# Products of the identity tile on TensorE while the modulation weights are loading

## The chip, the cores and the metric

The kernel runs on one core of one Trainium2 chip. The metric is the device time of one execution in microseconds (us); lower is better. In the profile the engines are PE (TensorE, the matrix engine; PEld are its weight loads), DVE (VectorE), ACT (ScalarE), POOL (GpSimd) and SP, which here only starts transfers.

## What is computed

One block with adaptive layer norm. A vector `c` gives six rows of 512 numbers (shift, scale and gate for each of two halves) through `silu(c) @ w_mod`. The first half is a state-space convolution over 2048 positions, the second a feed-forward layer with a squared ReLU.

```python
mod = (silu(c) @ w_mod)                       # 512 -> 6 x 512: sa, ca, ga, sb, cb, gb
h = layernorm(x) * (1 + ca) + sa              # x: 2048 x 512
K = real(sum_n C * exp(dt * A * l) * dt * B)  # 512 channels x 2048 positions, 128 states
y = irfft(rfft(h padded) * rfft(K padded))[:2048] + h * Dskip
x = x + ga * y
h = layernorm(x) * (1 + cb) + sb
x = x + gb * (square(relu(h @ w1 + b1)) @ w2 + b2)    # 512 -> 1792 -> 512
```

All values are float32. The identity tile that the change multiplies is not part of this; the kernel has it for transposes and for spreading a row over the partitions.

## The kernel before

The kernel has three stages. The **head** (to about 60 us) loads the parameters, makes `dt`, the step phases and the table entries, takes the statistics of the 16 row tiles of x (128 x 512 each), makes three of the modulation rows, and normalizes and re-sorts the row tiles. The **convolution** (to about 300 us) makes the kernel's spectrum from exponentials and sines, the transform of the input, their product, and the way back, in 8 groups of 64 channels. The **feed-forward** part takes the rest.

The lines of the head that the change and the prediction touch:

- L512: four products that spread `dt` over the partitions, TensorE's first work. L515 copies the result (ACT).
- L464: the loads of `w_mod`, 1 MB for each modulation row. L637 (`mod_rows`): the three groups of 16 products with them, for ga, ca and sa. L654 makes `gs4` from the first group, L655 `g4` from the second, L656 `s4` from the third (all DVE); L658 spreads `g4` over the partitions into the bank `kg`; L660 (ACT) and L661 (DVE) make `shift` from `s4`.
- L611 to L616: statistics of a row tile (DVE), and their last step for four tiles at a time (POOL).
- `row_pieces` (L673 to L683), 16 times: L673 (DVE) scales a row tile, L675 (ACT) makes the selecting tile `sel`, L677 and L680 (TensorE, one product and 16 column-tiled ones) write one of the three banks `ps`, and the copy L683 (ACT) empties it.
- `parameters` (L534 to L588), once for each half of the channels: a chain that goes to and fro between POOL (L535 to L542, L573 to L588), ACT (L544 to L546, L553, L554, L560 to L563, L570 to L572) and DVE (L534, L547 to L550, L555 to L567, L578). L558 is its reciprocal.
- L804 (ACT): the exponentials for the tables. `kgen_sin` (L823 to L825) writes sines into the two double banks `tg`; nothing uses these before.
- L717, L727, L857 and L875: the products of the convolution stage, column-tiled (64, 64, 32 and 64 columns of the array). L1050 are 32 x 32 tiles.

The order in which an engine takes its instructions isn't that of the code. `keep_order` (L168) puts the instructions into groups and walks through them with costs of its own (`weight`) and a clock of its own for TensorE; of the ready groups of an engine it takes the one with the longest way to the end, to which `urgent` adds a number. What it decides it fixes by dependencies. So an instruction that is added on one engine can change the order on the others. Its clock of TensorE:

```python
    WINDOW = 3413
    levels, busy = [0.5], {}
    ...
    def level(t):
        while len(levels) <= t // WINDOW:
            share = busy.get(len(levels) - 1, 0) / WINDOW
            levels.append(1.0 if share >= (0.475 if levels[-1] == 1 else 0.89) else 0.5)
        return levels[int(t // WINDOW)]
    ...
        g = first[e] if e == "SP" else max((g for g in ready[e] if at[g] <= now + 30), key=lambda g: to_end[g])
```

`whole` names instructions that form one group, `behind` holds pairs of which the second waits for the first. `bank("tg", 2)` hands out the two double banks in turn.

## Time and profile before

| | |
|---|---|
| median of 2 runs | 630.12 us (629.96 to 630.27) |
| the profiled execution | 628.47 us |
| its span, first to last instruction | 626.7 us |
| its mean granted clock of TensorE | 0.991 |
| PE, PEld busy | 575.5 us (92%), 489.7 us (78%) |
| DVE, ACT, POOL busy | 459.5 us (73%), 410.6 us (66%), 466.1 us (74%) |
| instructions | 21607 |

All times of a view are us from the span's start. A row of the timeline has the start, the length, the engine, line and operation, the tile written and the tiles read, how many instructions it merges, and in brackets the idle time ahead of it with what ended it. A product of float32 operands counts as two matmul records. In the page's line of slices each digit is a fortieth of the span (15.7 us) in tenths; PEclk is the clock that TensorE was granted. A row of the windows has a stretch, its length, and then the busy time of each engine.

### The profile page before, as it was taken

The page shows a single profiled execution, that of the slowest core. Times are in us where ns is not written, and L with a number is a line of the kernel's source. Part 1 is how long each engine was busy: PE and PEld are TensorE (multiplying, and loading weights), DVE is VectorE, ACT ScalarE, POOL GpSimd, SP SyncE. Part 2 cuts the span into 40 slices and gives each one's busy share as a digit, 9 for nine tenths or more (in the row PEclk, how much of TensorE's full clock was granted, in tenths as well). Part 3 has the DMA queues.
Part 4 walks back from the last instruction along what each step waited for, and adds up shares of the span by engine and source line. Part 5 has one row for each costly group of instructions (what it writes and reads, how often), then busy time and mean ns, then how long its engine had stood idle before and what let it go on. Part 6 is the DMA issues. An engine that isn't in the chain of part 4 may idle for free.

```text
span 626.7 us, 21607 instructions
## 1 busy us (share of the span) xinstructions
PE 575.5 (92%) x9390; PEld 489.7 (78%) x9390; DVE 459.5 (73%) x714; ACT 410.6 (66%) x780; POOL 466.1 (74%) x380
## 2 busy tenths in 40 slices
PE   1488999899999999998899799999998999999997
PEld 1355998899999999997767577788876887778885
DVE  6798779889688998757689944458999745456733
ACT  4938999979969877624785656545955655555441
POOL 6589799999998998240597997527999888761361
PEclk9979999999999999999999999999999999999999
DMA  8940104230311136255243332013534343211432
GB/s 317 396 150 4 68 5 99 43 70 11 64 38 38 22 86 155 54 174 152 71 121 85 97 111 78 17 35 100 152 118 157 113 121 108 57 35 33 136 100 84
DMA packets 45838, 60.70 MB, mean 97 GB/s; under 512 B 5168, under 2 KB 26544, under 8 KB 45616
## 3 DMA queue, kind: packets, MB, share of 16 engines
q1 hardware_dynamic: 45312, 59.20, 32.2%
q8 instruction: 73, 1.20, 0.8%
q10 hardware_dynamic: 432, 0.14, 0.1%
q14 instruction: 21, 0.17, 0.1%
HBM read 46.74 MB, written 4.19 MB: 81 GB/s over the span
## 4 chain that ended last, share of the span: by engine, by line
PE 50%; DVE 18%; POOL 12%; ACT 10%; issue 5%; DMA 4%; DVEq 0%; POOLq 0%; SPq 0%
PE ac L1165 8%; PE ps L875 6%; PE ps L717 5%; PE ps L727 5%; PE ps L1165 4%; PE ac L1186 3%; PE ac L1188 3%; PE ac L1187 3%; PE kg L857 3%; DVE r L1312 3%; DVE xy L867 2%; DVE p L1198 2%; DMA xy<-w 2%; DMA xy<-xt 2%; ACT tables L804 2%
## 5 line engine op out<-in xcount | busy, mean ns | idle before, releaser
L1134 POOL TENSOR_TENSOR w2r<-xy,w2r 128x512 fp32r<-128x512 f32 x56 | 81.2, 1450 | 68.4 <-ACT w2r L1133 68.4
L727 PE MATMUL ps<-xy,t_sb 128*64 128x64 f32 x2048 | 67.4, 223 | 0.6 <-issue 0.5
L727 PEld LDWEIGHTS ps<-xy,t_sb 128*64 128x64 f32 x2048 | 63.6, 138 | 3.4 <-issue 0.8
L875 PE MATMUL ps<-e_sb,xy 128*64 128x128 f32 (+2 forms) x1152 | 64.1, 266 | 2.2 <-ACT xy L719 1.7
L875 PEld LDWEIGHTS ps<-e_sb,xy 128*64 128x64 f32 x1152 | 58.8, 139 | 4.4 <-ACT xy L719 2.1
L1133 ACT CAST w2r<-xy 128x512 fp32r<-128x512 f32 x56 | 34.7, 620 | 24.3 <-DMA xy<-w 10.8
L719 ACT COPY xy<-ps 128x512 f32<-128x512 f32 x64 | 36.9, 589 | 14.8 <-PE ps L717 14.7
L1157 POOL TENSOR_TENSOR k1t<-xy,k1t 128x1024 fp32r<-128x1024 f32 x14 | 33.8, 2413 | 16.3 <-ACT k1t L1155 16.3
L1186 PE MATMUL ac<-w2r,r 128*128 128x512 f32 x112 | 43.8, 391 | 0.3 <-ACT big L1061 0.3
L1187 PE MATMUL ac<-w2r,r 128*128 128x512 f32 x112 | 43.6, 390 | 0.0
L1188 PE MATMUL ac<-w2r,r 128*128 128x512 f32 x112 | 43.6, 390 | 0.0
L837 POOL TENSOR_TENSOR rtl<-tables 128x1024 f32<-128x1024 f32 x22 | 43.4, 1972 | 0.2
L1165 PE MATMUL ac<-tt,k1t 128*128 128x512 f32 x168 | 42.0, 394 | 0.6
L867 DVE TENSOR_TENSOR xy<-ps,xy 128x512 f32<-128x512 f32 x64 | 39.3, 681 | 1.6 <-PE ps L727 1.1
L1165 PEld LDWEIGHTS ac<-tt,k1t 128*128 128x128 f32 x168 | 31.1, 188 | 9.2 <-DVE xy L1285 3.0
L813 POOL TENSOR_TENSOR rtl<-lo,big 128x1024 int32<-128x1024 int32 x16 | 34.3, 2145 | 3.3 <-ACT tg L825 2.6
L813 POOL TENSOR_TENSOR llph<-lo,big 128x1024 int32<-128x1024 int32 x16 | 34.5, 2158 | 1.4 <-ACT tg L825 1.4
L1187 PE MATMUL ps<-w2r,r 128*128 128x512 f32 x84 | 33.1, 395 | 1.9 <-POOL w2r L1134 1.8
L717 PE MATMUL ps<-d_sb,ksb 128*64 128x128 f32 x512 | 34.0, 274 | 0.6 <-DVE xy L867 0.5
L881 DVE COPY big<-ps 128x256 f32<-128x256 f32 (+1 forms) x66 | 24.0, 408 | 13.7 <-PE ps L875 13.6
L1186 PE MATMUL ps<-w2r,r 128*128 128x512 f32 x84 | 33.6, 400 | 0.0
L717 PE MATMUL ps<-d_sb,big 128*64 128x128 f32 x512 | 32.0, 274 | 1.1 <-ACT big L683 0.7
(276 smaller groups left out, 1684.8 us busy)
## 6 DMA issues: line engine op xcount, KB each, us to landing
xy<-w SPq DMA_DIRECT2D x91, 256.0 KB, 2.8
xy<-xt SPq DMA_DIRECT2D x32, 256.0 KB, 4.4
xy<-xy SPq DMA_DIRECT2D x32, 256.0 KB, 3.4
xy<-w_mod SPq DMA_DIRECT2D x6, 1024.0 KB, 8.5
out_dram<-p SPq DMA_DIRECT2D x16, 256.0 KB, 2.1
t_sb<-c_t SPq DMA_DIRECT2D x1, 2048.0 KB, 10.9
i2c<-c_i SPq DMA_DIRECT2D x4, 512.0 KB, 4.6
big<-prm SPq DMA_DIRECT2D x2, 768.0 KB, 5.8
```

The lines of the kernel that those rows point to most:

```text
L717: nc.tensor.matmul(ps[64 * r : 64 * r + 64, 128 * i : 128 * i + 128], src[:, i], d1_sb[:, r], start=True, stop=True)
L719: copy(dst[:, o // 4], ps.rearrange("p (t m) -> p m t", t=4))
L727: nc.tensor.matmul(ps[64 * r : 64 * r + 64, 64 * i : 64 * i + 64].rearrange("p (h q t) -> p q h t", h=2, t=2), t2_sb[:, 8 * g + i, r], src ...
L813: nc.gpsimd.tensor_tensor(ph.rearrange("p d r (a b) -> p (d r) a b", a=4), bc(low_phase[:, us].rearrange("p d r b -> p (d r) b"), 2, 4), b ...
L837: nc.gpsimd.tensor_mul(am[:, 0, :, 32:96].rearrange("p d (v x) -> p d v x", v=2), bc(et[:, 256 + 8 * d0 : 384 + 8 * d0].rearrange("p (y a) ...
L867: nc.vector.tensor_mul(product_piece(y, g), ps, piece(x, g))
L875: nc.tensor.matmul(ps[64 * m : 64 * m + 64], pairs(y)[:, g, i // 2, 64 * m : 64 * m + 64, i % 2], e1_sb[:, h].rearrange("p (r j) -> p r j" ...
L1134: nc.gpsimd.tensor_sub(to[:, 1], wst, to[:, 0].bitcast(F32))
L1165: nc.tensor.matmul(ps[:, cols], x, y, start=(i == 0 and not onto), stop=(i == 5), skip_group_check=onto)
L1186: pe.append(nc.tensor.matmul(banks[m], r2l[:, ms], hi_, start=(f == 0), stop=False))
L1187: pe.append(nc.tensor.matmul(banks[m], r2h[:, ms], lo_, start=False, stop=False))
L1188: pe.append(nc.tensor.matmul(banks[m], r2h[:, ms], hi_, start=False, stop=(f == NF - 1)))
```

## The change

Right behind L512, 54 products are issued in five forms: weights are a block of the identity tile, the moving operand is 64 columns of it, and the results go to the four banks of `tg`, which nobody reads. `warm(rows, cols, n)` goes n times over the array in tiles of `rows` x `cols`: 12 products of 64 x 128, 12 of 64 x 64, 6 of 128 x 128, 12 of 32 x 128 and 12 of 128 x 64. They wait for the last product of L512, each form is one group, and `urgent` ranks them behind everything else that is ready on TensorE.

```diff
     make_identity(nc, ident)
+
+    whole, in_turn, urgent, behind = {}, set(), {}, []
+    for _ in range(2):
+        bank("tg", 2)
+    banks = [t[:, 512 * i : 512 * i + 512] for t in rings["tg"][0] for i in range(2)]
+
...
     for i in range(4):
-        nc.tensor.matmul(
+        dtm = nc.tensor.matmul(
             dtp[:, 128 * i : 128 * i + 128], dtc[:, i : i + 1].to_broadcast([P, P]), ident, start=True, stop=True)
+
+    def warm(rows, cols, n):
+        for i in range(n):
+            for r in range(0, 128, rows):
+                for c in range(0, 128, cols):
+                    m = nc.tensor.matmul(
+                        banks[r // rows][c : c + cols, 64 * (i % 8) : 64 * (i % 8) + 64], ident[r : r + rows, c : c + cols],
+                        ident[r : r + rows, 0:64], start=True, stop=True).ins
+                    whole[m.name] = f"warm {rows} {cols}"
+                    behind.append((dtm.ins, m))
+                    urgent[m.name] = -1000000
+
+    for rows_, cols_, n in ((64, 128, 6), (64, 64, 3), (128, 128, 6), (32, 128, 3), (128, 64, 6)):
+        warm(rows_, cols_, n)
...
-    urgent, behind, paced = {}, [], []
+    paced = []
...
-    whole, in_turn = {}, set()
```

On TensorE they stand between L512 and the first L637, and the order of the rest of the head is the same there. On the other engines the order changes in places. The lines of the changed kernel are higher by 6 (L491 to L512) and by 20 (L515 to L1034), so L535 is L555 there.

DVE around the reciprocal, before. `gs` and `g` are the scaled modulation rows, `big` holds the parameters:

```order
L547 SCALAR_TENSOR_TENSOR big_86<-big_86 128x4x64
L555 SCALAR_TENSOR_TENSOR big_86<-big_86 128x4x64
L558 RECIPROCAL big_86<-big_86 128x4x64
L654 TENSOR_SCALAR gs_361<-ps_161 128x128
L548 SCALAR_TENSOR_TENSOR big_86<-big_86 128x4x64
L556 TENSOR_TENSOR big_86<-big_86 128x4x64
L655 SCALAR_TENSOR_TENSOR g_362<-ps_162,gs_361 128x128
L557 TENSOR_TENSOR big_86<-big_86 128x4x64
L559 TENSOR_TENSOR big_86<-big_86 128x4x64
```

The same place of DVE in the changed kernel:

```order
L567 SCALAR_TENSOR_TENSOR big_86<-big_86 128x4x64
L575 SCALAR_TENSOR_TENSOR big_86<-big_86 128x4x64
L674 TENSOR_SCALAR gs_417<-ps_163 128x128
L578 RECIPROCAL big_86<-big_86 128x4x64
L568 SCALAR_TENSOR_TENSOR big_86<-big_86 128x4x64
L576 TENSOR_TENSOR big_86<-big_86 128x4x64
L577 TENSOR_TENSOR big_86<-big_86 128x4x64
L675 SCALAR_TENSOR_TENSOR g_418<-ps_164,gs_417 128x128
L579 TENSOR_TENSOR big_86<-big_86 128x4x64
```

The read of the first modulation row has moved ahead of the reciprocal, and that of the second behind L577 (L557 before).

A little later on DVE, before, from the statistics of the ninth row tile (`xy_96`) on; `s` is `s4`:

```order
L611 BN_STATS st_75<-xy_96 128x6
L611 BN_STATS st_76<-xy_96 128x6
L612 BN_AGGR mv_74<-st_75 128x2
L612 BN_AGGR mv_74<-st_76 128x2
L611 BN_STATS st_77<-xy_96 128x6
L612 BN_AGGR mv_74<-st_77 128x2
L611 BN_STATS st_78<-xy_96 128x6
L612 BN_AGGR mv_74<-st_78 128x2
L656 TENSOR_TENSOR s_363<-ps_160,gs_361 128x128
```

And in the changed kernel:

```order
L631 BN_STATS st_75<-xy_96 128x6
L632 BN_AGGR mv_74<-st_75 128x2
L631 BN_STATS st_76<-xy_96 128x6
L632 BN_AGGR mv_74<-st_76 128x2
L693 SCALAR_TENSOR_TENSOR xy_94<-xy_94,mv_74,kg_421 128x512
L631 BN_STATS st_77<-xy_96 128x6
L631 BN_STATS st_78<-xy_96 128x6
L676 TENSOR_TENSOR s_419<-ps_162,gs_417 128x128
```

The scaling of the first row tile (L693, before L673) now stands here, ahead of `s4`; before, it came some 20 rows later, with the second and the third.

POOL behind the first product of the second half's parameters (L521), before; `mv` are the statistics:

```order
L521 TENSOR_TENSOR big_86<-big_86 128x4x64
L581 TENSOR_TENSOR big_86<-big_86 128x4x64
L577 TENSOR_TENSOR big_86<-big_86 128x4x64
L573 TENSOR_TENSOR big_86<-big_86 128x4x64
L574 TENSOR_TENSOR big_86<-big_86 128x4x64
L575 TENSOR_TENSOR big_86<-big_86 128x4x64
L615 TENSOR_SCALAR mv_74<-mv_74 128x4
L577 TENSOR_TENSOR big_86<-big_86 128x4x128 x3
L616 TENSOR_TENSOR mv_74<-mv_74,small 128x4
L535 TENSOR_TENSOR big_86<-big_86 128x4x64
L536 TENSOR_TENSOR big_86<-big_86 128x4x64
```

And in the changed kernel:

```order
L541 TENSOR_TENSOR big_86<-big_86 128x4x64
L555 TENSOR_TENSOR big_86<-big_86 128x4x64
L601 TENSOR_TENSOR big_86<-big_86 128x4x64
L597 TENSOR_TENSOR big_86<-big_86 128x4x64
L593 TENSOR_TENSOR big_86<-big_86 128x4x64
L594 TENSOR_TENSOR big_86<-big_86 128x4x64
L595 TENSOR_TENSOR big_86<-big_86 128x4x64
L635 TENSOR_SCALAR mv_74<-mv_74 128x4
L597 TENSOR_TENSOR big_86<-big_86 128x4x128 x3
L636 TENSOR_TENSOR mv_74<-mv_74,small 128x4
L556 TENSOR_TENSOR big_86<-big_86 128x4x64
```

L535 of before (now L555) has moved from behind the statistics to the second place, ahead of L581 (now L601).

In the convolution stage groups of TensorE change places with their neighbours (L857 with L717, L727 and L875), and rows of DVE, ACT and POOL with them; in the feed-forward stage TensorE's order is the same.

## The prediction

> **What bounds the kernel now.** I read the page first, for the shares of the engines and the slices, then the chain that ended last over the first 60 us, then TensorE alone over the same stretch.

> ```profile
> span 626.7 us, 21607 instructions
> PE 575.5 (92%) x9390; PEld 489.7 (78%) x9390; DVE 459.5 (73%) x714; ACT 410.6 (66%) x780; POOL 466.1 (74%) x380
> PE   1488999899999999998899799999998999999997
> PEclk9979999999999999999999999999999999999999
> ```

> TensorE is busy for 575.5 of 626.7 us, and only the first three or so slices (15.7 us each) are thin. From 60 us on it is the engine that everything waits for:

> ```profile
> 120.00:130.00 10.00, 10.00 (x332) 9.47 (x330) 9.87 (x18) 6.42 (x11) 10.00 (x8) 1.00 0.23 47
> 150.00:160.00 10.00, 10.00 (x310) 9.72 (x299) 9.69 (x15) 9.94 (x27) 9.61 (x11) 1.00 0.36 76
> ```

> Here the first busy number is PE (10.00 of 10.00 us), the last POOL. So a change in the first 50 us is worth what it moves the start of that dense stretch, and no more. What sets that start is in the chain (start, us, what):

> ```profile
> 8.00 0.59 ACT big L515
> 18.58 9.03 ACT tables L804 x48
> 32.56 0.74 POOL big L581
> 41.94 0.72 POOL big L535
> 46.43 0.74 POOL big L541
> 47.20 0.51 ACT big L544
> 49.12 0.48 ACT big L683
> 49.65 0.50 PE ps L677
> ```

> From 8 us to 49 us no product of TensorE is on the chain. ACT's exponentials, then POOL without a gap from 32.56, then ACT's phase steps hold back the copy L683, which frees the bank of the ninth row piece (L677 with L680). TensorE in the same stretch, with the idle time ahead of each row:

> ```profile
> 5.91 2.05 PE L512 MATMUL ps<-ident,dtc 128*128 128x128 f32 x8 [5.91 <-DVE dtc L509]
> 14.71 1.93 PE L637 MATMUL ps<-xy,srep 128*32 128x128 f32 x32 [6.75 <-DMA xy<-w_mod]
> 17.39 1.94 PE L637 MATMUL ps<-xy,srep 128*32 128x128 f32 x32 [0.74 <-DMA xy<-w_mod]
> 24.20 1.62 PE L637 MATMUL ps<-xy,srep 128*32 128x128 f32 x32
> 30.32 0.80 PE L677 MATMUL ps<-shift,pick 128*128 128x512 f32 x1 [4.50 <-DVE shift L661]
> 34.39 1.94 PE L680 MATMUL ps<-xy,big 128*32 128x128 f32 x32 [3.26 <-DVE xy L673]
> 45.11 1.08 PE L680 MATMUL ps<-xy,big 128*32 128x128 f32 x32
> 46.55 1.08 PE L680 MATMUL ps<-xy,big 128*32 128x128 f32 x32
> 49.65 0.50 PE L677 MATMUL ps<-shift,pick 128*128 128x512 f32 x1 [2.02 <-ACT big L683]
> ```

> The hole that the change fills is the 6.75 us ahead of 14.71. The same group L680 takes 1.94 us early and 1.08 us later: half clock and full clock, with a row piece every 1.44 us then (46.55 - 45.11). The windows give the switches (PE busy, granted clock, DMA share, GB/s):

> ```profile
> 28.50:29.00 0.50, 0.00 (x0) 0.78 0.85 360
> 39.00:39.50 0.50, 0.50 (x9) 0.98 1.06 393
> ```

> The clock falls at about 28.8, that is 3.0 us after TensorE stopped (24.20 + 1.62 = 25.8), and rises at about 39.0, 4.6 us after work resumed at 34.39. The 2.02 us hole at 47.6 did not drop it.

> **The added products.** 54 of them, two records each by the profile's count (L512: four products, x8), 108 records. Their price is not in this trace; from rows of other forms: L512 gives 0.256 us a record for a full tile and 128 columns at half clock; L637's 1.94/32 = 0.061 is a quarter of that, so four column tiles run side by side. With 64 columns instead of 128 a full tile costs between 0.128 (in proportion) and 0.256. The cheapest end, with row tiles side by side as well: 12 x 0.128 + 24 x 0.064 + 24 x 0.032 + 24 x 0.064 + 24 x 0.032 = 6.1 us at half clock. The dearest, 0.256 and no two row tiles at once: 12 x 0.256 + 24 x (0.256 + 0.128 + 0.256 + 0.128) = 21.5 us. The nearest rows are these, both 64 columns or several row tiles:

> ```profile
> 283.82 1.90 PE L1050 MATMUL ac<-big,i2c 32*32 32x128 f32 x128
> 71.38 1.10 PE L727 MATMUL ps<-xy,t_sb 128*64 128x64 f32 x32
> ```

> L727 costs 0.034 a record at full clock, so 64 columns go in proportion; L1050 costs 0.015, half of L680's 0.034 with four column tiles, so row tiles overlap too. I take 7 us. [...]

> They start at 5.91 + 2.05 = 7.96. With the 4.6 us of the one rise shown, the clock is up at about 10.5; by then 2.5 of the 7 us are done, and the other 4.5 shrink by 1.08/1.94 to 2.5: the end is at 13.0, ahead of w_mod's 14.71, and at 15.0 if the clock does not rise. Cost on the path: nothing; cover: the w_mod load.

> What a raised clock brings there: L637's first two groups shrink from 1.94 to 1.08. Nothing waits for them. The first is read by L654 on DVE, the second by L655, and both stood behind other DVE work:

> ```profile
> 18.14 1.75 DVE L558 RECIPROCAL big<-big 128x256 f32<-128x256 f32 x1
> 19.81 0.23 DVE L654 TENSOR_SCALAR gs<-ps 128x128 f32<-128x128 f32 x1
> 21.86 0.28 DVE L655 SCALAR_TENSOR_TENSOR g<-ps,gs 128x128 f32<-128x128 f32 x1
> 29.58 0.42 DVE L564 SCALAR_TENSOR_TENSOR big<-big 128x256 f32<-128x256 f32 x1 [1.35 <-ACT big L561]
> 33.51 2.05 DVE L673 SCALAR_TENSOR_TENSOR xy<-xy,mv,kg 128x512 f32<-128x512 f32 x3
> ```

> The groups ended at 16.64 and 19.33, their readers began at 19.81 and 21.86. So the warming as such I cost at 0. The clock is lost again before it matters: with g at about 22.3 (0.4 later, since L557 now stands ahead of it), L658 and the third L637 end near 26, and L677 waits for ACT until 30.3, a hole over the 3.0 us that dropped it before.

> **The moved instructions** are what is left, since the planner, which now believes in a fast TensorE, has dealt the rows anew. On POOL, L535 (now L555) leaves the gapless stretch and goes ahead of L581 (now L601):

> ```profile
> 28.46 0.72 POOL L521 TENSOR_TENSOR big<-big 128x256 f32<-128x256 f32 x1 [0.35 <-DMA big<-prm]
> 32.56 0.73 POOL L581 TENSOR_TENSOR big<-big 128x256 int32<-128x256 int32 x1 [3.38 <-ACT big L571]
> ```

> POOL stands idle for 3.38 us there with L535's operands on hand (L521, the row before, waited for the same load). That takes 0.72 us out of the chain between 32.56 and 47.20. Against it: on DVE the first row's L673 (now L693) goes ahead of s4 (0.68 us, 2.05/3) into the stretch that had 1.35 us to spare at 29.58, and the shift row (0.34) now stands ahead of L564. The spare time takes the first, the second reaches L567 and so L581 with 0.1 to 0.3 us. Net gain on the chain: 0.72 - 0.2 = **0.5 us**. DVE's swaps of L654 with L558 and of L655 with L557 leave the same instructions ahead of L559, which ACT waits for: nothing.

> The early row starts the row pieces at 31.1 instead of 34.39. Piece 0 ends at 33.1, piece 1 waits for its own row until 34.4 and ends at 36.3, piece 2 (0.80 + 1.94) at 39.1, five more at 1.44 each at 46.3, against 47.63 before. The ninth still waits for the copy behind ACT's phase steps, now at 49.15. So these 1.3 us turn into idle time: a hole of about 2.85 us instead of 2.02.

> **Behind 60 us**, DVE, ACT and POOL rows and some groups of TensorE (L857 against L717 and L875) change places between about 115 and 300 us; nothing is added. TensorE is full there, so only its few holes can change:

> ```profile
> PE ps L875 <- ACT xy L719: 1.7, 1, 1.7
> PE kg L857 <- issue: 0.7, 1, 0.7
> PE ac L1050 <- issue: 1.9, 2, 1.4
> q8 instruction: 73, 1.20, 0.8%
> ```

> The first could close (-1.7), a like one could open (+2). The 108 records are less than one more packet of q8 (9390/73 = 129 records each) and shift where its packets end by some 20 records; the holes put down to issue bound that at -1.4 to +1.4. I take 0 for both and keep -2.2 to +2.2 for the range.

> **Sum** against the profiled execution, 628.47 us (span 626.7 and 1.8 around it): 0 for the products, 0 for the clock, -0.5 for POOL, 0 behind: 628.0. The median before is 630.12, 1.65 above that execution; I carry the difference to it: **629.6**.

> **The rivals.**

> *The clock drops in the longer hole.* TensorE idle for 3.0 us dropped it, 2.02 did not; 2.85 lies near the former. The next pieces would then run as the early ones, 0.80 + 1.94 instead of 0.50 + 1.08, for up to the 4.6 us of the rise shown: a loss of 4.6 x (1 - 1.58/2.74) = 1.9, so 630.12 - 0.5 + 1.9 = 631.5. Against it: one fall is all that the trace shows, and 2.85 is shorter than its 3.0. [...]

> *The products outlast the load and hold DVE: slower.* L654 now stands ahead of the reciprocal, so DVE stops if the first L637 is not done by 18.1. With 1.94 for that group the point is an end of the products after 16.2; the slack of 0.7 us left ahead of L564 moves it to about 16.9, and from there each us is a us on the chain. At the dear end with the clock up at 11: 8.0 + 3 + 18.5 x 0.56 = 21.4, then 1.08: DVE held 4.3, minus slack 0.7 and gain 0.5: +3.1, 633.2; without any rise the products end at 29.5, +12, 642. The rows L727 and L1050 speak against it.

> *The new order opens or closes holes behind 60 us*: 629.6 + 2.2 = 631.8, or 629.6 - 2.2 = 627.4. POOL's share there (9.6 of 10) says that a late POOL row reaches TensorE soon; that TensorE is full says that little is to be had.

> *It doesn't raise the clock*, because tiled products count for too little activity: L637 stays at 1.94 at 14.71, no reader waits, and the time is the same 629.6.

> **Numbers.** 629.6 as summed, with or without the rise: 0.46. Clock drop, 631.5: 0.27. Holes open, 631.8: 0.10; holes close, 627.4: 0.10. Products too long: 0.07. The likeliest case with its issue term spans 628.2 to 631.0; the range takes in the drop and both kinds of holes and a part of the long products: 626.6 to 633.2. Two per cent, 12.6 us, is about what a measurement of this kernel tells from no change; no case but the extreme of the long products comes near it: faster 0.01, same 0.97, slower 0.02.

> **What would show it.** The added products between 8 and 14 us, L637 (now L657) at about 1.1 us; L601 on POOL near 32.7 and L564's row on ACT (before L544) near 46.7; the first L680 (now L700) at about 31; the hole ahead of the ninth piece near 2.8 us, with the clock at 1.00 or 0.50 behind it; the dense stretch of the same length. I am wrong if L658 or the reciprocal waits for TensorE at 18 to 24 us, or if TensorE has new holes between 115 and 300 us.

## The result and the profile after

The changed kernel takes **636.62 us** (636.25 to 636.99, two runs) against 630.12: a ratio of 1.0103, with a 95% interval of 1.0060 to 1.0147. It is slower by 6.5 us (3.8 to 9.3 by the interval), less than the two per cent but outside the predicted range of 626.6 to 633.2. The profiled execution took 636.25 us, its span is 634.5 us against 626.7.

The head of the page, as it was shown of before (span, busy time of the engines, slices of TensorE and its granted clock):

```profile
span 634.5 us, 21828 instructions
PE 590.6 (93%) x9498; PEld 503.2 (79%) x9498; DVE 454.9 (72%) x714; ACT 412.4 (65%) x780; POOL 469.2 (74%) x380
PE   6688998999989998999889899999998999999997
PEclk9778998999999999999899899999999999999999
```

The 108 records are there (9498 - 9390). TensorE is busier by 15 us, of which the products are 9.4. In the slices the first two digits go from 1 and 4 to 6 and 6. In the convolution the 7th goes from 9 to 8 and the 8th from 8 to 9 (95 to 127 us), and the 12th and 16th (174 to 190 and 238 to 254 us) go from 9 to 8. First the head, in TensorE's timeline:

```profile
7.88 9.39 PE L525 MATMUL tg<-ident 64*128 64x64 f32 x108
17.20 3.61 PE L657 MATMUL ps<-xy,srep 128*32 128x128 f32 x64
22.94 1.16 PE L678 MATMUL kg<-g,ident 128*128 128x128 f32 x8 [2.13 <-DVE g L675]
24.03 1.93 PE L657 MATMUL ps<-xy,srep 128*32 128x128 f32 x32
49.90 0.50 PE L697 MATMUL ps<-shift,pick 128*128 128x512 f32 x1 [2.36 <-ACT big L703]
52.06 1.94 PE L700 MATMUL ps<-xy,big 128*32 128x128 f32 x32
```

The products ran without a gap from 7.88 to 17.2 and hold the first two groups with `w_mod` back from 14.7 to 17.20. These two take 3.61 us together: 1.94 is the half-clock price of one, so the clock rose only near the end of the second. The first record of the granted clock in this trace is the rise at 20.65; the views print 1.00 for all the time before it, so up to there the clock is read from the length of the rows. At 24.03 it is lost again, as the 1.93 shows, and a second time behind the hole at 49.90. Now the convolution, in windows of 10 us (the first busy number is PE, the last POOL, then the granted clock):

```profile
150.00:160.00 10.00, 8.64 (x319) 7.98 (x317) 8.99 (x17) 6.86 (x10) 9.61 (x9) 1.00 0.15 31
170.00:180.00 10.00, 8.39 (x236) 7.72 (x224) 8.45 (x14) 9.91 (x16) 8.29 (x7) 1.00 0.01 3
230.00:240.00 10.00, 8.68 (x274) 8.34 (x272) 9.97 (x17) 6.62 (x9) 9.69 (x9) 1.00 0.02 3
250.00:260.00 10.00, 8.54 (x252) 8.02 (x254) 8.38 (x13) 9.07 (x12) 9.09 (x7) 1.00 0.29 94
```

The same windows before, where the first is already shown with 10.00:

```profile
170.00:180.00 10.00, 9.95 (x326) 9.26 (x324) 9.07 (x18) 7.04 (x10) 9.30 (x7) 1.00 0.02 3
230.00:240.00 10.00, 10.00 (x312) 9.58 (x310) 8.92 (x16) 4.76 (x9) 8.17 (x6) 1.00 0.42 88
250.00:260.00 10.00, 10.00 (x336) 9.58 (x334) 9.85 (x18) 6.68 (x11) 4.04 (x3) 1.00 0.10 32
```

TensorE now stands idle for 1.3 to 1.6 us in each of the four windows, at full clock. Its rows with longer idle time between 75 and 260 us say for whom it waits:

```profile
102.32 1.79 PE L877 MATMUL kg<-llph 128*32 128x64 f32 x64 [2.69 <-DVE ksb L959]
151.49 2.08 PE L747 MATMUL ps<-xy,t_sb 128*64 128x64 f32 x64 [0.69 <-DVE big L901]
159.51 1.09 PE L747 MATMUL ps<-xy,t_sb 128*64 128x64 f32 x29 [0.67 <-issue]
180.10 3.02 PE L747 MATMUL ps<-xy,t_sb 128*64 128x64 f32 x96 [1.69 <-ACT xy L739]
239.42 1.97 PE L895 MATMUL ps<-e_sb,xy 128*64 128x128 f32 x32 [1.32 <-DVE xy L887]
252.46 0.42 PE L877 MATMUL kg<-rtl 128*32 128x64 f32 x8 [1.46 <-issue]
```

The longest of them, 2.69 us at 102.32, adds nothing to the lateness: the kernel before had holes of 0.75, 0.52 and 1.67 us between 100 and 112 us, and these are gone. The other five are what is new; before, the longest between 115 and 260 us is one of 0.51.

Matching TensorE's instructions of the two profiles one by one, the changed kernel is 1.7 us late from 60 to 140 us apart from a stretch around 100, 3 to 4.5 between 160 and 220, 7.6 at 250, and 7.8 at the end. So the profile puts 1.7 us in the head and 6 us between 140 and 250 us, in the stage where the change adds nothing.

### The profile page after: what moved, and what is told of

Read it like the earlier page. It is cut to its first block, busy times and chain, and to the rows that moved or that the text cites. A ratio compares the mean times of both kernels' runs of the same rounds, so it can differ in the third digit from the quotient of the medians.

```text
span 634.5 us, 21828 instructions
## 1 busy us (share of the span) xinstructions
PE 590.6 (93%) x9498; PEld 503.2 (79%) x9498; DVE 454.9 (72%) x714; ACT 412.4 (65%) x780; POOL 469.2 (74%) x380
## 4 chain that ended last, share of the span: by engine, by line
PE 45%; DVE 18%; POOL 17%; ACT 8%; issue 6%; DMA 4%; DVEq 0%; SPq 0%; POOLq 0%; ACTq 0%
PE ac L1183 8%; PE ps L747 4%; PE ps L1183 4%; PE ps L737 4%; PE ac L1204 3%; PE ac L1206 3%; PE ac L1205 3%; PE ps L895 3%; DVE r L1330 3%; PE kg L877 2%; ACT tables L824 2%; DVE p L1216 2%; POOL big L1082 2%; POOL rtl L857 2%; PE kg L1183 2%
## 5 line engine op out<-in xcount | busy, mean ns | idle before, releaser
L857 POOL TENSOR_TENSOR rtl<-tables 128x1024 f32<-128x1024 f32 x22 | 43.3, 1970 | 0.2
L1183 PEld LDWEIGHTS ac<-tt,k1t 128*128 128x128 f32 x168 | 31.1, 188 | 9.2 <-DVE xy L1303 3.0
L833 POOL TENSOR_TENSOR llph<-lo,big 128x1024 int32<-128x1024 int32 x16 | 34.5, 2154 | 5.2 <-ACT tg L845 5.2
L833 POOL TENSOR_TENSOR rtl<-lo,big 128x1024 int32<-128x1024 int32 x16 | 34.4, 2148 | 5.3 <-ACT tg L845 4.6
L901 DVE COPY big<-ps 128x256 f32<-128x256 f32 (+1 forms) x66 | 24.3, 409 | 16.6 <-PE ps L895 14.7
L1205 PE MATMUL ps<-w2r,r 128*128 128x512 f32 x84 | 33.1, 395 | 1.8 <-POOL w2r L1152 1.8
```

The source lines that it names most:

```text
L833: nc.gpsimd.tensor_tensor(ph.rearrange("p d r (a b) -> p (d r) a b", a=4), bc(low_phase[:, us].rearrange("p d r b -> p (d r) b"), 2, 4), b ...
L857: nc.gpsimd.tensor_mul(am[:, 0, :, 32:96].rearrange("p d (v x) -> p d v x", v=2), bc(et[:, 256 + 8 * d0 : 384 + 8 * d0].rearrange("p (y a) ...
L1183: nc.tensor.matmul(ps[:, cols], x, y, start=(i == 0 and not onto), stop=(i == 5), skip_group_check=onto)
L1205: pe.append(nc.tensor.matmul(banks[m], r2h[:, ms], lo_, start=False, stop=False))
```

## The experiments

Two theories stood first. **O**: the order that the planner (`keep_order`) dealt anew is what costs. **R**: the 108 additional records shift where TensorE's instruction packets end (the page's queue q8 has 73 packets before and 74 with them), and the stalls for the next packet then fall on worse places. In all runs below the kernel before ran on the same chip; its medians there were 628.9 to 629.9, single runs 626.9 to 635.0.

### Products without the new order, and the new order without the products

All products run, but the planner gives them no time and no records, so every engine has the order of before:

```diff
+    unseen = {g for g, il in enumerate(groups) if whole.get(il[0].name, "").startswith("warm")}
+    for g in unseen:
+        takes[g] = [0, 0]
...
-        if e == "PE":
+        if g in unseen:
+            pass
+        elif e == "PE":
```

> All 108 added records are issued, but the planner gives them no time and no records, so every other instruction stands in the order of before. Theory O (the loss lies in the new order): within 1.5 us of before, since the products end before anything that waits for them. Theory R (the loss lies in the records: they move the ends of the instruction packets, and with them the holes put down to issue): 4 to 6 us slower than before, with issue holes as in the changed kernel.

Measured: 629.29 us, ratio 1.0006 (0.9987 to 1.0024).

The reverse: one product of each form runs, five in all, and the planner counts each for all of its form, so that the order is that of the changed kernel:

```diff
+    stands_for = {}   # group of a product -> how many it stands for
...
-            n, t = sum(map(records, groups[g])), now
+            n, t = stands_for.get(g, 1) * sum(map(records, groups[g])), now
...
-        for i in range(n):
-            for r in range(0, 128, rows):
-                for c in range(0, 128, cols):
+        for i in (n - 1,):
+            for r in (128 - rows,):
+                for c in (128 - cols,):
```

> 5 products (10 records) instead of 54 (108), while the planner counts all 54: the order of the changed kernel, nearly without its products. Theory O: about 6 us slower than before, like the changed kernel. Theory R: within 1.5 us of before.

Measured: 638.38 us, ratio 1.0140 (1.0102 to 1.0177). The products cost nothing measurable, nor does the shift of 108 records; the order costs all of it. R falls.

### Which part of the order

Both run all products, walk the plan twice (without and with the products) and splice the two orders on every engine where the head ends, at the first group that reads `d1_sb`:

```diff
+    plain, shifted = walk(False), walk(True)
...
+        queues[e] = s[:k] + p[k:]      # e3_head; e3_late has p[:k] + s[k:]
```

> All products; the order of the changed kernel in the head (up to the first L717 of TensorE), the order of before from there. If the head's new order costs what its trace shows at 62 us, 1.6 us slower than before; if the head is free and the convolution's order costs, within 1 us of before.

Measured: 629.28 us, ratio 1.0003 (0.9983 to 1.0023).

> All products; the order of before in the head, the order of the changed kernel from the first L717 on. If the convolution's order costs, 4 to 6 us slower than before; if the records' shift costs whatever the order, as much as the run with the products alone.

Measured: 637.09 us, ratio 1.0129 (1.0089 to 1.0168). The new order of the head, with the early first row, POOL's moved L555 and the longer hole, is worth nothing measurable in either sense. The late part costs 8 us.

The late part differs in three stretches, with the same groups in each on every engine, and they were run one by one: `e6_A` (140 to 210 us), `e6_B` (210 to 255 us) and later `e6_C` (270 to 300 us). Some rows of DVE, ACT and POOL between about 70 and 115 us have changed places as well. These were not run alone, but by 115 us `e3_late` is no later than the kernel before.

```diff
+    span = {
+        "PE": [(103, 161)],
+        "DVE": [(219, 308)],
+        "Activation": [(163, 231)],
+        "Pool": [(117, 165)],
+        "SP": [(40, 48)],
+    }
...
+        for a, b in span[e]:
+            queues[e][a:b] = s[a:b]
```

> All 108 products run. The order is that of the kernel before except between 140 and 210 us (one stretch of the convolution, 58 of TensorE's groups, 89 of VectorE's, 68 of ScalarE's), where it is that of the changed kernel. Theory 'sum of places' (the cost of the late order is a sum of a few separate places, each an instruction that stands ahead of one which TensorE needs sooner): this stretch gave +2.4 us of lag in the profile of e3_late (from -1.23 before 140 us to +1.16 at 180 to 200), made of a hole on TensorE of 0.82 at 149.9 and one of 1.69 at 178.5; so +2.4 us over the kernel before, about 631.5 if that is 629.1 here. Rival 'spread' (the late order as a whole is tighter or looser, no single place counts, what is lost in a stretch is waited for later anyway): under +1, or the whole +8.

Measured: 632.20 us, ratio 1.0057 (1.0036 to 1.0077). The ratio makes it +3.6 us on the 629.9 there, the medians +2.3. This rests on its six times (631.03 to 635.11): the profiled execution was the fastest of them, and its lag behind `e1_products_only`, 2.2 at 210 to 240 us, is 0.7 at 250 and gone by 400.

> All 108 products run. The order is that of the kernel before except between 210 and 255 us (the next stretch: 45 of TensorE's groups, 73 of VectorE's, 55 of ScalarE's), where it is that of the changed kernel. Theory 'sum of places': this stretch gave +2.9 us of lag in the profile of e3_late (from 0.42 at 210 to 3.3 at 250), so +2.9 over the kernel before, about 632.0. Rival 'carried over' (the stretch is only slow because it starts late and out of step, after the stretch at 140 us): under +1.

Measured: 634.16 us, ratio 1.0077 (1.0058 to 1.0096), +4.9 us by the ratio and +4.2 by the medians.

> All 108 products run; the order of before except between 260 and 300 us (20 rows of VectorE, 10 of ScalarE, 3 of GpSimd, none of TensorE), where it is that of the changed kernel. If the loss is the sum of the stretches: e3_late +8.1, less e6_A's +3.6 and e6_B's +4.8, leaves -0.3: within 1 of the kernel before; by the lag in e3_late's profile there (3.7 at 270, 4.8 at 300) +1.

Measured: 630.24 us, ratio 0.9999 (0.9968 to 1.0031). Two stretches carry the loss, and the third carries none. By the ratios A and B add up to 8.5 against the +8.1 of `e3_late`, by the medians to 6.5 against 8.2, so they make up all or most of it; the rivals "spread" and "carried over", with under +1 for a stretch, fall. In stretch B the trace shows what goes with it. Before (`e1_products_only`, whose lines are those of before plus 25), TensorE makes a group of kernel rows `kg<-rtl` at 212, and `kg<-llph` at 221:

```profile
211.99 1.12 PE L882 MATMUL kg<-rtl 128*32 128x64 f32 x64
221.24 1.12 PE L882 MATMUL kg<-llph 128*32 128x64 f32 x64
```

In `e6_B` (lines of before plus 46) that first group stands behind five more, and the windows of 5 us have the rest (PE, PEld, DVE, ACT, POOL):

```profile
212.54 3.02 PE L773 MATMUL ps<-xy,t_sb 128*64 128x64 f32 x96 [0.49 <-ACT xy L765]
220.74 1.12 PE L903 MATMUL kg<-rtl 128*32 128x64 f32 x64
223.86 1.12 PE L903 MATMUL kg<-llph 128*32 128x64 f32 x64
236.95 1.97 PE L921 MATMUL ps<-e_sb,xy 128*64 128x128 f32 x32 [1.36 <-DVE xy L913]
...
220.00:225.00 5.00, 4.89 (x178) 4.30 (x176) 1.92 (x6) 2.00 (x3) 3.46 (x3) 1.00 0.78 174
235.00:240.00 5.00, 3.64 (x88) 3.33 (x86) 5.00 (x9) 1.86 (x3) 3.14 (x3) 1.00 0.40 84
```

The kernel rows come 8.7 us later (220.74 against 211.99). DVE and ACT are then busy for 1.92 and 2.00 of 5 us at 220 (4.33 and 4.69 in `e1_products_only`), and at 235 DVE is full (5.00 of 5.00, against 4.46) while TensorE waits for it. The lag of `e6_B` against `e1_products_only` goes from -0.5 at 215 to +3.1 at 250 and stays at about 3.2 to the end. This is what the trace shows beside the loss; that this one group's place is the cause was not tested alone.

### Putting single instructions back

In stretch A the trace of `e3_late` offered two instructions that wait ahead of others: on ScalarE the second copy of `kg`, which waits 2.7 us for TensorE ahead of the burst of exponentials, and on VectorE a sum that waits for POOL ahead of two copies. Both were moved back, one after the other:

```diff
+    act = queues["Activation"]
+    act[175], act[176] = act[176], act[175]                # e7_A_copy and e8_A_copy_sum
+    dve = queues["DVE"]
+    dve[221:224] = [dve[222], dve[223], dve[221]]          # e8_A_copy_sum
```

> As e6_A, with one instruction moved by one place: on ScalarE the second copy ksb<-kg behind the sines, which in the changed order stands ahead of the burst of 24 exponentials and waits there 2.68 us for TensorE's kg, goes behind the burst. Theory 'sum of places': the burst starts at about 154.7 instead of 157.4, the sines behind it and the copies xy<-ps come 2.7 earlier, TensorE's hole of 1.69 at 178.5 goes: 1.7 under e6_A, about +0.7 over the kernel before. Rival 'TensorE's or GpSimd's own order' (it is the kg products put behind the two groups before them, or GpSimd's additions in another order): as e6_A within 0.5.

Measured: 638.97 us, ratio 1.0148 (1.0127 to 1.0168).

> As e7_A_copy, with one more instruction moved by two places: on VectorE the 1024-wide sum llph<-llph,tg, which in the changed order stands ahead of two copies big<-ps and waits there 0.83 us for GpSimd, goes behind them. Theory 'sum of places': TensorE's hole of 0.82 at 149.9 goes as well: 0.8 under e7_A_copy, within 0.5 of the kernel before. Rival: as e7_A_copy.

Measured: 639.08 us, ratio 1.0160 (1.0138 to 1.0183). The theory of separate places fell, and badly: the first move does not give 1.7 us back, it costs about 6 more (6.8 by the medians, 5.7 by the ratios), and the second changes nothing. The rival of the first, no change, fell too. ScalarE's and TensorE's timelines of `e7_A_copy` show what happens (lines of before plus 48):

```profile
160.11 5.84 ACT L852 ACTIVATE tables<-big 128x128 f32<-128x128 f32 x24 [2.35 <-POOL rtl L885]
165.71 0.45 ACT L986 COPY ksb<-kg 128x256 f32<-128x256 f32 x1
...
166.50 1.75 PE L905 MATMUL kg<-llph 128*32 128x64 f32 x64 [2.52 <-DVE ksb L987]
170.53 1.98 PE L765 MATMUL ps<-d_sb,ksb 128*64 128x128 f32 x16 [2.28 <-DVE big L929]
```

The burst (L852) could not have started earlier: it overwrites `tables`, which POOL's L885 reads until 160.07 (158.12 + 1.95), because POOL too has a new order. So the copy's wait was all but free, and behind the burst it keeps `kg` full, TensorE stands for 2.52 and 2.28 us, and after that its rows run at half clock (1.98 for x16, as against 1.04 at full). In the changed order ScalarE's late copy and POOL's late reads belong together. In POOL's rows, before:

```profile
150.54 0.71 POOL L789 TENSOR_TENSOR lo<-lo,big 128x256 int32<-128x256 int32 x1
152.22 1.97 POOL L837 TENSOR_TENSOR rtl<-tables 128x1024 f32<-128x1024 f32 x1
```

and in the changed kernel, with two more sums for `tables` (L809, before L789) and a phase step (L833) ahead of the reads:

```profile
152.22 2.25 POOL L809 TENSOR_TENSOR lo<-lo,big 128x256 int32<-128x256 int32 x3
154.55 2.14 POOL L833 TENSOR_TENSOR rtl<-lo,big 128x1024 int32<-128x1024 int32 x1
157.66 1.96 POOL L857 TENSOR_TENSOR rtl<-tables 128x1024 f32<-128x1024 f32 x1
```

The same read of `tables` ends at 159.62 instead of 154.19: 5.4 us later, and 3.8 with the 1.7 taken off that the kernel is late anyway. The burst of the changed kernel starts at 160.38, 0.8 us behind that end, so without the copy's wait it could have gained no more than this.

### One engine's order put back

With every engine's order known for both kernels, they were mixed engine by engine over the three stretches (`queues[e]` from `shifted` on the engines named, from `plain` on the others).

> All 108 products run. In the stretches at 140 to 255 and 270 to 300 us VectorE, ScalarE and GpSimd keep the changed order, and TensorE alone goes back to the order of before (it differs at about a dozen places, above all four groups of kg<-rtl or kg<-llph that the changed order puts behind one to six other groups). Theory P (TensorE's kg products are late, so the kernel rows and all that is made of them are late): most of the +8 goes, within +2 of the kernel before, about 631. Theory Q (GpSimd does the sums for tables ahead of the phase additions, which holds ScalarE's burst): as e3_late within 1.5, about +6.5 to +8, 637. Theory J (each engine's order only suits the others', so a mix is no better than the whole): as e3_late or slower, 637 or more.

Measured: 649.68 us, ratio 1.0323 (1.0298 to 1.0348).

> As e9_pe_before, but GpSimd alone goes back to the order of before and TensorE, VectorE and ScalarE keep the changed one. P: as e3_late, +6.5 to +8. Q: most of it goes, within +2, about 631. J: as e3_late or slower.

Measured: 647.90 us, ratio 1.0300 (1.0271 to 1.0329).

> As e9_pe_before, and GpSimd too goes back to the order of before: only VectorE and ScalarE keep the changed order. P: as e9_pe_before, within +2. Q: within +2. J: as e3_late or slower. A theory V (VectorE's and ScalarE's own order costs): +6 to +8.

Measured: 657.24 us, ratio 1.0436 (1.0411 to 1.0462).

> All 108 products run, the order of before on every engine but GpSimd, which has the changed order in those stretches (24 rows). P: 0 to +1, about 630. Q: +4 to +8, 634 to 638. J: anything from +2 up.

Measured: 645.76 us, ratio 1.0244 (1.0222 to 1.0266). P, Q and V all fall, and J holds: each of the four mixes is slower than the whole new order, so neither TensorE's nor POOL's part is the loss by itself. VectorE's and ScalarE's parts were run together only. Of the mix with POOL's changed rows alone, TensorE's longest waits:

```profile
160.61 1.15 PE L773 MATMUL ps<-xy,t_sb 128*64 128x64 f32 x32 [3.09 <-DVE xy L913]
185.57 5.50 PE L773 MATMUL ps<-xy,t_sb 128*64 128x64 f32 x128 [4.31 <-ACT xy L765]
239.25 3.68 PE L921 MATMUL ps<-e_sb,xy 128*64 128x128 f32 x32 [5.84 <-ACT xy L765]
```

Behind each of these holes the clock is lost as well (5.38 us for a group of 3.67, 5.50 for one of 3.90 and 3.68 for one of 1.97), which adds to the price of a mix. What stays open is which of the differing places in stretch A and B the loss would go with if one could be moved alone: the orders of the engines fit each other, and the two single moves that were tried gave nothing back.

### Is this order an especially bad one?

Three theories were left: **L**, any shift of the planner's count draws another order, and these lie some per cent apart; **M**, the count of 108 misleads it; **N**, all but one are within 1 us. The planner again does not see the products, and only begins its count of records at another number:

```diff
-    done_records, end, asked, queued = 0, FIRST_END, None, []
+    done_records, end, asked, queued = 48, FIRST_END + (PACKET if 48 > FIRST_END else 0), None, []
```

> All 108 products run; the planner does not see them, but starts its count of TensorE's instruction records at 24 instead of 0, and deals the rows from that: 24 rows of difference to the order of before on TensorE, 74 on VectorE, 65 on ScalarE, 19 on GpSimd. Theory L (any shift of the count draws another order, and the orders lie some per cent apart): anywhere from -3 to +10 us of the kernel before, without a trend over the four numbers. Theory M (it is the count of 108 that misleads the planner): near the kernel before, 0 to +2. A third, N (the planner's own model puts up with any shift, and orders of this kind are all within 1 us but for the one bad one): within 1 us.

Measured: 634.24 us, ratio 1.0084 (1.0055 to 1.0113).

> As e10_shift24 with 48. L: -3 to +10, unrelated to the run with 24. M: +2 to +4. N: within 1 us.

Measured: 636.51 us, ratio 1.0116 (1.0084 to 1.0148).

> As e10_shift24 with 72 (the order differs in about twice as many rows: 56, 120, 121 and 48). L: -3 to +10, unrelated to the others. M: +4 to +6. N: within 1 us.

Measured: 637.97 us, ratio 1.0160 (1.0096 to 1.0225).

> As e10_shift24 with 96 (40, 98, 106 and 33 rows). L: -3 to +10, unrelated to the others. M: +6 to +8. N: within 1 us.

Measured: 634.98 us, ratio 1.0114 (1.0052 to 1.0176). Each number gave another order on all four engines, and each order is slower, by 0.8 to 1.6 per cent, with no rise towards 108: N and M fall. L's spread is there, but only on one side. The order of before lies at the good end of six (these four, its own and that of the changed kernel); the changed one is an ordinary member of the rest. Why the order of before is the good one is not shown. It is not that its packet ends fit those on the chip: in `e1_products_only` 108 records more run ahead of the same order, and the time is the same.

The products bring three things into the walk: their time, their activity (which raises its clock of TensorE) and their records. Which of them dealt the rows anew in the changed kernel is not shown. These four runs show that another count of records is enough. It isn't needed: in the orders as they are built, without a run, the products' time alone, with neither activity nor records, gives another order too, and so do time and activity without the records.

### Products that do raise the clock

> The order of before on every engine, as in e1_products_only, and each of the 108 records moves 128 columns of the identity instead of 64. Theory A (a record takes 213 ns at half clock because of its weight load, and the clock did not rise because the array rests while weights load): the products take 9.4 us or a little more if the clock does not rise, up to 11 us where 128 columns take 0.256 us as in L512's row, and as the array now works nearly all the time, the clock rises within them, some 4 to 7 us after their start, and the first w_mod products take 1.1 us each instead of 1.9. Rival B (small tiled products never count enough, whatever they move): no rise before the w_mod products. For the time both say within 1 us of the kernel before, since nothing waits there; over +1 if the products last past 19 us and hold VectorE's read of the first modulation row.

Measured: 629.76 us, ratio 0.9994 (0.9963 to 1.0025). TensorE's timeline (lines of before plus 25):

```profile
8.74 6.87 PE L530 MATMUL tg<-ident 64*128 64x128 f32 x108
15.54 1.08 PE L662 MATMUL ps<-xy,srep 128*32 128x128 f32 x32
17.47 1.08 PE L662 MATMUL ps<-xy,srep 128*32 128x128 f32 x32 [0.84 <-DMA xy<-w_mod]
25.11 1.94 PE L662 MATMUL ps<-xy,srep 128*32 128x128 f32 x32
```

Twice the columns take 6.87 us instead of 9.39, since the clock rises among them, and both first groups take 1.08. At 25.11 it is gone again, and the time is that of before. Theory A holds in that the clock rises, but earlier than its 4 to 7 us: the first record of the granted clock is at 9.97, 1.2 us after the products start. In the 17 kept traces that run all the products with 64 columns it is never before their end (at 17.97 to 22.33). The columns make the difference, and not how full a stretch is: from 6.56 to 9.97 TensorE is busy for 0.94 of the time here, from 6.67 to 10.09 in `e6_C` for 0.95, and there the clock does not rise. Why the narrow products count for less is not shown.

## Why the prediction was wrong, step by step

**The step that failed is "Behind 60 us ... I take 0 for both", with -2.2 to +2.2 for the range.** It measured about +8 (`e3_late` +8.1, of which `e6_A` and `e6_B` make up all or most). The places were named rightly, L857 against L717 and L875, and "new holes between 115 and 300 us" is what was said would show it wrong. The size failed for two reasons. The bound came from the holes that the trace of before had, the largest single one 1.7 and one like it; but a new order has no reason to open just one hole, and here there are five of 0.7 to 1.7 between 150 and 255 us. The hole that "could close" did close, and one of 2.69 opened 10 us ahead of it. And TensorE at 10.00 of 10.00 was read as "little is to be had", which holds for a gain; for a loss the same rows say the opposite: with POOL at 9.6 to 10.0 and DVE at 9.7 to 9.9 there is little to absorb a late row. That this is why the other orders are slower is argued, not tested. The rival "opens holes" had the mechanism at 0.10, and its 631.8 was too small by 5 us.

**"The planner, which now believes in a fast TensorE"** is not shown to be the cause: a shift of its count of records alone dealt four other orders. The prediction priced the 108 records as packets on the chip, at -1.4 to +1.4 (measured: ratio 1.0006), and did not ask what they do in the walk.

**The products**: cost nothing measurable, as forecast. Their duration was not: 9.4 us, above the 7 taken and inside the 6.1 to 21.5 of the bounds. By form:

```profile
L525 PE MATMUL tg<-ident 64*128 64x64 f32 x24 | 2.8, 422 | 0.0
L525 PE MATMUL tg<-ident 128*128 128x64 f32 x12 | 2.8, 425 | 0.0
L525 PE MATMUL tg<-ident 128*64 128x64 f32 x24 | 1.5, 318 | 0.0
```

A full tile costs 2.8/12 = 0.23 a record, not 0.128: "64 columns go in proportion" was read from L727, whose weights are 64 columns wide. The forms with 128 columns of weights gain nothing from the narrower moving operand: from the start of one record to that of the next it is 0.213 us in L512 with 128 moving columns, and 0.213 here with 64. The prediction's 0.256 for L512 was its 2.05 us over eight, with the longer first and last record in it. A change of tiling had no row that gave its price; here, where one form ends and the next begins, 0.24 to 0.35 us lie between two starts. That two row tiles run side by side was right (2.8/24 = 0.117, half of a full tile), and with half the columns of weights as well as two column tiles a record costs 1.5/24 = 0.063, a quarter. A load took 327, 329 and 321 ns in the forms with 128 columns of weights and 64, 128 and 32 rows, and 223 and 215 in those with 64 columns and 128 and 64 rows. The rival "products outlast the load" put its point at an end after 16.2. The end was 17.2, and DVE did wait:

```profile
19.20 0.29 DVE L674 TENSOR_SCALAR gs<-ps 128x128 f32<-128x128 f32 x1 [1.10 <-PE ps L657]
30.02 0.95 DVE L584 SCALAR_TENSOR_TENSOR big<-big 128x256 f32<-128x256 f32 x1
33.20 0.74 POOL L601 TENSOR_TENSOR big<-big 128x256 int32<-128x256 int32 x1 [2.51 <-DVE st L631]
47.45 0.51 ACT L564 ACTIVATE big<-big,magic 128x256 f32<-128x256 f32 x1 [3.28 <-POOL big L561]
```

**The clock**: "up at about 10.5" was wrong by 10 us (20.65), and the rival "doesn't raise the clock" was right in what came, but not in its reason: the products of `e11_wide` are tiled in the same way and raise it. That neither changes the time was right, which `e11_wide` shows with the clock raised.

**POOL's -0.5** did not come. L601 starts at 33.20 instead of 32.7, and L564 at 47.45 instead of 46.7 (47.20 before). The shift row ahead of it makes DVE's L584 0.44 us late (30.02 instead of 29.58), and it took 0.95 instead of 0.42 beside the moved POOL row (L555, 29.85 to 30.69). That is 0.9 us by L587 (32.07 instead of 31.17), where the prediction had 0.1 to 0.3, and L587 holds ACT's L590 and L591, for which L601 waits (before, the view names this row, L571, for the wait; here it names a DVE row that ended later). That the 1.10 us ahead of L674 reached no further is not shown; the whole head costs nothing measurable in `e3_head`.

**The hole ahead of the ninth piece** grew to 2.36 instead of 2.85, since the clock rose at 41.1 and not by 39 and the eighth piece ended at 47.54 and not at 46.3. The rival "clock drops" did happen in this execution (L700 at 52.06: 1.94). `e3_head` has the same order there, its clock fell behind 2.23 us of idleness, and yet its median is that of before. In `e3_late` a hole of 2.24 left the clock up. `e3_head` first, then `e3_late` (lines of before plus 41 in both):

```profile
51.04 0.50 PE L718 MATMUL ps<-shift,pick 128*128 128x512 f32 x1 [2.23 <-ACT big L724]
52.95 1.94 PE L721 MATMUL ps<-xy,big 128*32 128x128 f32 x32
```

```profile
49.68 0.50 PE L718 MATMUL ps<-shift,pick 128*128 128x512 f32 x1 [2.24 <-ACT big L724]
51.55 1.08 PE L721 MATMUL ps<-xy,big 128*32 128x128 f32 x32
```

So the threshold that the prediction looked for between 2.02 and 3.0 isn't one of length: what counts besides is where the hole lies. In all 20 kept traces the 198 records of the granted clock lie whole multiples of 3.41 us apart (25.37, 28.78, 39.02 and 626.11 us in the trace of before). Each of the 99 falls ends such a stretch of 3.41 us in which TensorE was busy for 0.62 of the time or less; above 0.62 there is none, and between 0.44 and 0.62 the clock fell or stayed (in the changed kernel it fell at 0.44 and stayed at 0.47). The hole of 2.69 us at 102.32 in the changed kernel lies in one stretch (99.15 to 102.57, busy for 0.73 us), and the clock falls at its end. A hole of the same 2.69 us in `e3_late` (up to 100.68) lies across two (2.12 and 2.02 us busy), and it stays. In `e11_wide` a hole of 1.73 us was enough. So the "3.0 us after TensorE stopped" and the "4.6 us after work resumed" were not delays, but where the ends of these stretches fell: the fall at 28.78 and the rise at 39.02 lie three of them apart.

## What to carry to other kernels

Where a planner deals the order, an instruction that costs nothing on the chip still enters its walk, and a shift of any of its counts can deal another order; if the order at hand is a good one, expect a loss and price it by how far such orders lie apart (here 0.8 to 1.6 per cent), not by the holes of the profile at hand. Keep helpers that nobody waits for out of the planner's counts. A wait in a trace is not a cost until something behind it could have run: of a new order one instruction put back cost about 6 us more.
